# A two-stage attention and token-mixing kernel: token mix in two column parts, q loaded first, the root on Pool in the first batch, mixers turned at landing, and a new timetable

## The chip, the cores and the metric

The kernel runs on one core of one Trainium2 chip. The metric is the device time of one execution in microseconds (us). "PE" is TensorE's matmul stream, "DVE" is VectorE, "ACT" is ScalarE, and "POOL" is GpSimd.

## The reference, cut to what matters

```python
# attention without softmax: B = 8, H = 8, S = 576, D = 64
kv  = einsum('bhsd,bhse->bhde', k, v)
out = einsum('bhsd,bhde->bhse', q, kv)
x   = out / sqrt(mean(out**2, -1) + 1e-6) * g_norm      # then (B, S, 512)
# mixing of phases
theta = x @ w_theta
y  = w_tok_r @ (x * cos(theta)) + w_tok_i @ (x * sin(theta))   # over the 576 tokens
u  = x + y
result = u + maximum(u @ w_ch, 0)
```

## The kernel before

Each batch goes through seven stages. They are written as generators. A list of start times and steps (the timetable) sorts their pieces by a nominal time, and each engine gets its instructions in exactly that order. The nominal times themselves are never waited for, so the timetable is nothing but an order for each engine's queue.

```python
START = [8.0, 38.0, 60.0] + [86.0 + 26.0 * i for i in range(5)]
STEPS = {                      # stage: (offset from the batch's start, step from tile to tile)
    "cast": (-1.0, 3.4), "attention": (0.0, 3.4), "norm": (16.0, 5.2), "turn": (24.0, 5.2),
    "phase": (28.0, 5.2), "mix": (54.0, 3.25), "channel": (82.0, 5.2),
    # ... own entries for the first batch
}
PS = {"kv": 1, "raw": 2, "tp": 2, "mm": 3}            # PSUM banks by use
```

The stages that the argument needs, cut:

```python
def norm(b, ti):                 # one tile of 128 tokens, 5 tiles (the last of 64)
    # PE: raw (PSUM) ...; ACT: sq = raw**2; then
    nc.vector.reduce_sum(out=ss, in_=sq)
    if b > 0:                    # first batch: one chain of 13 instructions on VectorE, for all tiles
        nc.gpsimd.tensor_scalar(out=ss, in0=ss, scalar1=D * eps, op0=ALU.add)
        nc.gpsimd.tensor_tensor(out=rt, in0=ss, in1=mhalf, op=ALU.pow)
    yield 2.8
    nc.vector.tensor_tensor(out=x, in0=raw, in1=rt, op=ALU.mult)

def phase(b, ti):                # PE: th = x @ w_theta; ACT: pt; DVE: f, fa; ACT: tr = sin; DVE: z
    ...

def mix(b, i):                   # 8 groups of 9 matmuls
    (kc, half) = divmod(i, 2)    # the half (288 of 576 tokens) is the inner loop
    # PE: y (PSUM, "mm"); DVE: uT = y * g + xT, for 128 channels and one half
    ...

def channel(b, ti):              # needs uT of all 512 channels for tile ti
    # PE: ups (transpose) and vps = u @ w_ch ("mm"); ACT: u; DVE: ot = max(vps, 0) + u; store
    ...
```

Because the half is the inner loop of the mix, no channel tile can run before the seventh of the eight mix groups. The middle tile straddles both halves and needs all eight.

Of the kernel before, what the change touches and what calls it, by code (L numbers as in the profile page):

```python
# [10 lines left out]
FP32 = mybir.dt.float32  # L11
# [8 lines left out]
START = [8.0, 38.0, 60.0] + [86.0 + 26.0 * i for i in range(5)]  # L20
STEPS = {
    "cast": (-1.0, 3.4),
    "attention": (0.0, 3.4),
    "norm": (16.0, 5.2),
    "turn": (24.0, 5.2),
    "phase": (28.0, 5.2),
    "mix": (54.0, 3.25),
    "channel": (82.0, 5.2),

    ("norm", 0): (14.5, 0.4),  # L30
    ("turn", 0): (22.0, 0.9),
    ("phase", 0): (24, 1.2),
    ("mix", 0): (36.0, 2.6),
    ("channel", 0): (60.0, 4.0),
}

# [18 lines left out]
def kernel(  # L55
# [31 lines left out]
    SH = S // 2  # L87
# [51 lines left out]
    loaded = {}  # L139

    def load(b):
# [3 lines left out]
        for hp in range(HP):  # L145
# [4 lines left out]
            for (dst, src) in ((kt, k), (vt, v), (qt, q)):  # L150
                nc.sync.dma_start(
                    out=dst[:].rearrange("p h j d -> p h (j d)"),
                    in_=src[b, pair, 0:SF, :].rearrange("h (p j) d -> p h (j d)", j=NF),
                )
# [33 lines left out]
    def cast_theta(kc):  # L188
        nc.scalar.activation(out=wth[:, kc, :], in_=wst_t[kc][:], func=AFT.Copy, scale=FOLD)

    def mixer_tails():
        for i in range(2):
            nc.gpsimd.tensor_copy(wtt[:, 0:NF, i, :], wnat[i][:, :, SF:S])
            nc.gpsimd.tensor_copy(wtt[:T, NF, i, :], wnatl[i][:, SF:S])

    def load_mixers():

        nc.gpsimd.tensor_copy(late[:], loaded[0][2][HP - 1][:, 0, 0, 0:1])  # L198
        for (i, src) in ((0, moe_w_tok_r), (1, moe_w_tok_i)):
# [3 lines left out]
            nc.gpsimd.dma_start(out=wnatl[i][:], in_=src[SF:S, :])  # L203
        nc.gpsimd.dma_start(out=wch[:], in_=moe_w_ch.rearrange("(k p) c -> p k c", p=P))

    def mixer_step(n):

        pw = ps("tp", [P, S], FP16, f"wTps{n}")
        for tj in range(NT):
            rows = P if tj < NF else T  # L210
            if n < 2 * NF:
                i = n // NF
                src = wnat[i][:, tj, :] if tj < NF else wnatl[i][:, :]
                st = src[:, bass.ds(n % NF, P, NF)]
            else:
                st = wtt[:rows, tj, :, :]
            nc.tensor.matmul(  # L217
                pw[:, tj * P:tj * P + rows], st, ident16[:rows, :rows],
# [11 lines left out]
    st = {}  # L230

    def cast_q(b, hp):
# [5 lines left out]
        if hp == 0:  # L238
            nc.vector.tensor_copy(qc[:T, NF], ql[:])
        yield 0  # L240

    def attention(b, hp):
        (ks, vs, qs, kl, vl, ql) = loaded[b]
        if hp == 0:
            st["kv", b] = ps("kv", [P, HP, D], FP32, f"kv{b}")
        kvp = st["kv", b]
        pair = slice(2 * hp, 2 * hp + 2)
# [8 lines left out]
        pq = ps("tp", [P, SX], FP16, f"qTps{b}_{hp}")  # L256
        for j in range(NT):
            nc.tensor.matmul(  # L258
                pq[:, j * P:(j + 1) * P], qcast[b % 2][:, j, pair, :], ident16[:],
                is_transpose=True, start=(j == 0), stop=(j == NT - 1),  # L260
            )
        yield 2.0
        t = work.tile([P, S], FP16, tag="qT", bufs=2 * HP, name=f"qT{b}_{hp}")
        nc.scalar.copy(out=t[:], in_=pq[:, 0:S])  # L264
# [9 lines left out]
    def rsqrt(rt, ss, n):  # L274

        i = work.tile([P, n], I32, tag="rs_i", name="rs_i")
        h = work.tile([P, n], FP32, tag="rs_h", name="rs_h")
        w = work.tile([P, n], FP32, tag="rs_w", name="rs_w")
        nc.vector.tensor_scalar(
            out=ss, in0=ss, scalar1=D * eps, scalar2=None, op0=ALU.add  # L280
        )
        nc.vector.tensor_scalar(
            out=i[:], in0=ss.bitcast(I32), scalar1=1, scalar2=None,
            op0=ALU.logical_shift_right,
        )
        nc.vector.tensor_scalar(
            out=rt.bitcast(I32), in0=i[:], scalar1=-1, scalar2=0x5F3759DF,
            op0=ALU.mult, op1=ALU.add,
        )
        nc.vector.tensor_scalar(  # L290
            out=h[:], in0=ss, scalar1=-0.5, scalar2=None, op0=ALU.mult
        )
        for _ in range(3):
            nc.vector.tensor_tensor(out=w[:], in0=rt, in1=rt, op=ALU.mult)
            nc.vector.tensor_tensor(out=w[:], in0=w[:], in1=h[:], op=ALU.mult)
            nc.vector.scalar_tensor_tensor(
                out=rt, in0=w[:], scalar=1.5, in1=rt, op0=ALU.add, op1=ALU.mult
            )

    def norm(b, ti):  # L300


        first = b == 0
        bd = kv_bd[b % 2]
        raw = ps("mm" if first and ti >= 2 else "raw", [P, C], FP32, f"raw{b}_{ti}")
# [14 lines left out]
        if ti == 0 or not first:  # L320
            n = NT if first else 1
            tag = "0" if first else ""
            st["ss", b] = work.tile(
                [P, n, H], FP32, tag="ss" + tag, bufs=4 - 3 * first, name=f"ss{b}_{ti}"
            )
            st["rt", b] = work.tile(
                [P, n, H], FP32, tag="rt" + tag, bufs=4 - 3 * first, name=f"rt{b}_{ti}"
            )
        ss, rt, at = st["ss", b], st["rt", b], ti if first else 0
        nc.vector.reduce_sum(  # L330
            out=ss[:, at], in_=sq[:].rearrange("p (h e) -> p h e", h=H),
            axis=mybir.AxisListType.X,
        )
        if not first:
            nc.gpsimd.tensor_scalar(  # L335
                out=ss[:, 0], in0=ss[:, 0], scalar1=D * eps, scalar2=None, op0=ALU.add
            )
            nc.gpsimd.tensor_tensor(out=rt[:, 0], in0=ss[:, 0], in1=mhalf[:], op=ALU.pow)  # L338
            yield 2.8
        else:  # L340
            if ti == NT - 1:
# [188 lines left out]
```

## Time and profile before

| | before |
|---|---|
| time, median of 3 | 266.01 us (264.6 to 266.35) |
| profiled span | 265.8 us |
| PE, DVE, ACT, POOL busy | 226.2, 192.4, 165.4, 77.3 us |

These are lines of the page of the kernel before. The first has busy time, share and count of instructions. The next two have 40 equal slices of the span, with PE's busy share and the granted PE clock in tenths. The last has the shares of the chain that ended last, by engine.

```profile
PE 226.2 (85%) x2253; PEld 153.3 (58%) x2253; DVE 192.4 (72%) x408; ACT 165.4 (62%) x291; POOL 77.3 (29%) x88
...
PE   1472886998867798899999998999899979889993
PEclk9999997799999999999999999999999999999999
...
PE 35%; DVE 28%; POOL 13%; ACT 9%; DMA 6%; issue 6%; SPq 1%; POOLq 1%; ACTq 0%; DVEq 0%
```

The fill, the first 60 us or so, has the holes.

The next lines are busy times by stage. A stage ends when another batch's worth of mix matmuls (72) has been issued; the first ends at the first batch's first mix group, and the ninth at the last matmul. The columns are the window, its length, busy us (with instructions) of PE, PEld (weight loads), DVE, ACT and POOL, then the granted clock, the DMA share and GB/s.

```profile
0.00:47.50 47.50, 27.47 (x260) 19.49 (x261) 25.51 (x70) 23.59 (x41) 6.64 (x18) 0.96 1.04 263
47.50:88.40 40.90, 34.89 (x405) 23.93 (x405) 26.75 (x54) 26.37 (x47) 14.92 (x16) 0.97 0.47 144
88.40:111.50 23.10, 19.50 (x207) 13.21 (x204) 20.19 (x45) 16.32 (x29) 9.91 (x10) 1.00 0.99 269
111.50:135.70 24.20, 23.94 (x266) 16.99 (x265) 20.34 (x43) 18.33 (x32) 9.83 (x10) 1.00 0.21 70
135.70:163.30 27.60, 27.38 (x287) 18.55 (x285) 22.73 (x48) 19.93 (x37) 10.15 (x10) 1.00 0.63 182
163.30:190.50 27.20, 26.27 (x281) 18.12 (x277) 22.97 (x48) 19.66 (x36) 10.15 (x10) 1.00 0.62 175
190.50:216.80 26.30, 25.36 (x254) 16.98 (x252) 22.08 (x45) 19.43 (x36) 9.51 (x10) 1.00 0.14 46
216.80:240.70 23.90, 21.00 (x165) 13.17 (x162) 19.59 (x40) 15.40 (x27) 6.16 (x7) 1.00 0.15 50
240.70:261.00 20.30, 20.22 (x153) 12.87 (x152) 11.52 (x20) 6.38 (x11) 0.00 (x0) 1.00 0.30 101
```

The Trainium skill says, in "Perfetto Trace Analysis", "Per-instruction lifecycle": the end of a matmul is estimated by the profiler and not observed. For this reason I count **lost** time as the length of a stage less its work at dense pace. The dense paces are read from start to start of groups in the timeline: mix group of 288 columns 1.10 us; theta or channel group 0.86; k-v group 0.73; transposes of q 0.37, of a mixer 0.46, others 0.22; raw 0.22.

The first batch's norm on VectorE, from its timeline (start, length, engine, line, operation):

```profile
22.66 0.68 DVE L330 TENSOR_REDUCE ss_0_287<-sq_4_302 128x8 f32<-128x512 f32 x1
...
26.36 0.69 DVE L346 TENSOR_TENSOR x_0_327<-raw_0_261,rt_0_288 128x512 f16<-128x512 f32 x1
...
31.54 0.69 DVE L382 SCALAR_TENSOR_TENSOR f_0_379<-pt_0_371,th_0_355 128x512 f32<-128x512 f32 x1 [2.10 <-ACT pt_0_371 L379]
```

The chain of 13 small instructions, cut here, stands between the last reduce and the first x at 26.36 us; it starts at 23.37 us. The first f comes at 31.54 us.

### The profile page before, as it was taken

To read this page: it belongs to the slowest core of one execution; us is meant where nothing else is said; L and a number is where in the kernel's file an instruction comes from. 1 tells how busy PE (TensorE), PEld (TensorE's weight loads), DVE (VectorE), ACT (ScalarE), POOL (GpSimd) and SP (SyncE) were. 2 spreads that over 40 slices of the span, in tenths; PEclk is the share of its full clock that TensorE was granted. 3 is DMA by queue.
4 is the path that set the end of the run, shared out by engine and by line. 5 is a ranking of instruction groups with operands and counts; after the bars stand their busy time and mean duration, and the time that the engine had idled before them with its cause. 6 is when DMAs were issued, how large, how long until landed. Compare 5 with 4: busy or idle time off the path is not lost.

```text
span 265.8 us, 5776 instructions
## 1 busy us (share of the span) xinstructions
PE 226.2 (85%) x2253; PEld 153.3 (58%) x2253; DVE 192.4 (72%) x408; ACT 165.4 (62%) x291; POOL 77.3 (29%) x88
## 2 busy tenths in 40 slices
PE   1472886998867798899999998999899979889993
PEld 1361455686534575577667665767666646556651
DVE  5118567347688978887978789778987888786552
ACT  2146496234997798378856885688568857752231
POOL 2051000023553353532252423343334423500000
PEclk9999997799999999999999999999999999999999
DMA  5999999886221899631239911993121112122234
GB/s 158 284 362 211 247 343 224 274 234 206 78 79 42 198 313 257 205 120 42 79 112 247 316 43 43 229 333 111 41 62 42 41 39 61 40 79 62 79 100 141
DMA packets 45676, 41.04 MB, mean 154 GB/s; under 512 B 15056, under 2 KB 40272, under 8 KB 45648
## 3 DMA queue, kind: packets, MB, share of 16 engines
q1 hardware_dynamic: 44608, 38.81, 50.4%
q0 software_dynamic: 1040, 1.85, 3.7%
q8 instruction: 18, 0.29, 0.5%
q14 instruction: 10, 0.08, 0.1%
HBM read 33.06 MB, written 9.44 MB: 160 GB/s over the span
## 4 chain that ended last, share of the span: by engine, by line
PE 35%; DVE 28%; POOL 13%; ACT 9%; DMA 6%; issue 6%; SPq 1%; POOLq 1%; ACTq 0%; DVEq 0%
DMA ql_111<-in_q_dram 2%; DMA v_3_134<-in_v_dram 2%; DMA out_dram<-ot_0_2607 1%; DVE ss_0_287 L330 1%; PE kv_463 L250 1%; PE y_0_604 L420 1%; PE kv_1985 L250 1%; PE kv_1522 L250 1%; POOL rt_4_1365 L338 1%; DVE uT_2529 L425 1%; POOL rt_3_2640 L338 1%; POOL rt_1_2883 L338 1%; POOL rt_1_1486 L338 1%; POOL rt_1_2416 L338 1%; POOL rt_4_1009 L338 1%
## 5 line engine op out<-in xcount | busy, mean ns | idle before, releaser
L335 POOL TENSOR_SCALAR ss_0_704<-ss_0_704 128x8 f32<-128x8 f32 x1 | 0.2, 240 | 27.7 <-DVE ss_0_704 L330 27.7
L258 PEld LDWEIGHTS <-qcast_75 128*128 128x128 f16 x80 | 5.3, 106 | 3.3 <-DVE qcast_75 L235 1.6
L258 PEld LDWEIGHTS <-qcast_77 128*128 128x128 f16 x80 | 4.8, 100 | 4.0 <-DVE qcast_77 L235 2.9
L359 PE MATMUL xTps_0_338<-ident_79,x_0_327 128*128 128x128 f16 x4 | 0.6, 305 | 5.7 <-DVE x_0_327 L346 5.7
L250 PE MATMUL kv_155<-vl_68,kl_67 128*64 128x64 f32 x16 | 1.8, 319 | 3.6 <-DMA vl_68<-in_v_dram 3.6
L250 PE MATMUL kv_155<-v_0_113,k_0_112 128*64 128x64 f32 x16 | 1.1, 319 | 4.3 <-DMA v_0_113<-in_v_dram 4.3
L264 ACT COPY qT_0_200<-qTps_0_166 128x576 f16<-128x576 f16 x1 | 0.6, 639 | 6.6 <-PE qTps_0_166 L258 6.6
L198 POOL COPY late<-q_3_135 128x1 f32<-128x1 f32 x1 | 0.4, 438 | 13.6 <-DMA q_3_135<-in_q_dram 13.6
L359 PEld LDWEIGHTS <-x_0_327 128*128 128x128 f16 x4 | 0.3, 130 | 5.9 <-DVE x_0_327 L346 5.9
L250 PEld LDWEIGHTS kv_155<-vl_68,kl_67 128*64 128x64 f32 x16 | 1.4, 222 | 3.7 <-issue 3.7
L250 PEld LDWEIGHTS kv_155<-v_0_113,k_0_112 128*64 128x64 f32 x16 | 1.0, 222 | 4.3 <-DMA k_0_112<-in_k_dram 4.3
L373 PEld LDWEIGHTS <-xT_337 128*128 128x128 f16 x20 | 2.2, 120 | 2.1 <-issue 1.1
L330 DVE TENSOR_REDUCE ss_0_287<-sq_0_271 128x8 f32<-128x512 f32 x1 | 0.7, 686 | 3.6 <-ACT sq_0_271 L318 3.6
L373 PEld LDWEIGHTS <-xT_3332 128*128 128x128 f16 x20 | 1.9, 98 | 2.2 <-issue 0.9
L364 ACT ACTIVATE xT_337<-xTps_0_338,gcol 128x512 f16<-128x512 f16 x1 | 0.7, 687 | 3.4 <-PE xTps_0_338 L359 3.4
L217 PEld LDWEIGHTS <-wnat_107 128*128 128x128 f16 x16 | 1.5, 123 | 2.3 <-issue 2.1
L373 PEld LDWEIGHTS <-xT_1108 128*128 128x128 f16 x20 | 1.8, 98 | 1.6
L373 PEld LDWEIGHTS <-xT_2426 128*128 128x128 f16 x20 | 1.9, 98 | 1.3
L373 PEld LDWEIGHTS <-xT_2893 128*128 128x128 f16 x20 | 1.9, 98 | 1.3
L373 PEld LDWEIGHTS <-xT_1496 128*128 128x128 f16 x20 | 1.9, 98 | 1.3
L373 PEld LDWEIGHTS <-xT_1954 128*128 128x128 f16 x20 | 1.9, 98 | 1.3
L441 PEld LDWEIGHTS <-uT_1584 128*128 128x128 f16 (+1 forms) x20 | 1.8, 100 | 1.4 <-issue 0.2
(1950 smaller groups left out, 985.6 us busy)
## 6 DMA issues: line engine op xcount, KB each, us to landing
wnat_106<-in_moe_w_tok_r_dram POOLq DMA_DIRECT2D x1, 576.0 KB, 8.6
wnat_107<-in_moe_w_tok_i_dram POOLq DMA_DIRECT2D x1, 576.0 KB, 10.9
kl_67<-in_k_dram SPq DMA_DIRECT2D x4, 128.0 KB, 5.2
vl_68<-in_v_dram SPq DMA_DIRECT2D x4, 128.0 KB, 5.5
kl_71<-in_k_dram SPq DMA_DIRECT2D x4, 128.0 KB, 5.5
vl_72<-in_v_dram SPq DMA_DIRECT2D x4, 128.0 KB, 6.5
wch<-in_moe_w_ch_dram POOLq DMA_DIRECT2D x1, 512.0 KB, 13.8
k_0_112<-in_k_dram SPq DMA_DIRECT2D x1, 256.0 KB, 2.8
```

The costliest lines, as they stand in the source:

```text
L217: nc.tensor.matmul(pw[:, tj * P:tj * P + rows], st, ident16[:rows, :rows], is_transpose=True, start=(tj == 0), stop=(tj == NT - 1),)
L250: nc.tensor.matmul(kvp[r * D:(r + 1) * D, hp, :], ks[hp][:, r, j, :] if j < NF else kl[:, 2 * hp + r, :], vs[hp][:, r, j, :] if j < NF els ...
L258: nc.tensor.matmul(pq[:, j * P:(j + 1) * P], qcast[b % 2][:, j, pair, :], ident16[:], is_transpose=True, start=(j == 0), stop=(j == NT - 1),)
L264: nc.scalar.copy(out=t[:], in_=pq[:, 0:S])
L330: nc.vector.reduce_sum(out=ss[:, at], in_=sq[:].rearrange("p (h e) -> p h e", h=H), axis=mybir.AxisListType.X,)
L338: nc.gpsimd.tensor_tensor(out=rt[:, 0], in0=ss[:, 0], in1=mhalf[:], op=ALU.pow)
L359: nc.tensor.matmul(px[:, kc, :], st["x", b, ti][:, kc * P:(kc + 1) * P], ident16[:], is_transpose=True, start=(kc == 0), stop=(kc == NK - 1),)
L364: nc.scalar.activation(out=st["xT", b][:, :, ti * P:(ti + 1) * P], in_=px[:], func=AFT.Copy, scale=gcol[:],)
L373: nc.tensor.matmul(th[:], xT[:, kc, ti * P:(ti + 1) * P], wth[:, kc, :], start=(kc == 0), stop=(kc == NK - 1),)
L420: nc.tensor.matmul(y[:], st["z", b, m][:, kc * P:(kc + 1) * P], wT[m][:, cols], start=(m == 0), stop=(m == 2 * NF),)
L425: nc.vector.scalar_tensor_tensor(out=st["uT", b][:, kc, cols], in0=y[:], scalar=gcol[:], in1=st["xT", b][:, kc, cols], op0=ALU.mult, op1=A ...
L441: nc.tensor.matmul(vp[:rows], uT[:, kc, ti * P:ti * P + rows], wch[:, kc, :], start=(kc == 0), stop=(kc == NK - 1),)
```

## The change

The intent, as the diff shows it, is to let channel tiles of a batch run before its mix is complete (first the columns of 256 tokens for all channels, then those of 320), to shorten the first batch's start, and to give all queues a new order. The core of the diff:

```diff
-START = [8.0, 38.0, 60.0] + [86.0 + 26.0 * i for i in range(5)]
+START = [8.0, 33.0, 54.1, 80.3, 106.3, 132.5, 158.4, 184.5]
 STEPS = {
-    "cast": (-1.0, 3.4), "attention": (0.0, 3.4), "norm": (16.0, 5.2), "turn": (24.0, 5.2),
-    "phase": (28.0, 5.2), "mix": (54.0, 3.25), "channel": (82.0, 5.2),
+    "cast": (-3.73, 2.84), "attention": (-0.20, 3.37), "norm": (16.34, 5.20), "turn": (23.12, 5.34),
+    "phase": (27.31, 5.11), "mix": (54.00, 3.16), "channel": (70.95, 4.96),
+    ("channel", 0): (47.00, 4.14), ("channel", 1): (59.52, 5.04),   # ... and more for batches 0 and 1
 }
+MIXERS = (17.68, 1.09)            # the mixers' turns stood at 28.0, 0.8
@@ mix
-    SH = S // 2
+    SH = 2 * P
-        (kc, half) = divmod(i, 2)
+        (half, kc) = divmod(i, NK)
@@ load and attention
-            for (dst, src) in ((kt, k), (vt, v), (qt, q)):
+            for (dst, src) in ((qt, q), (kt, k), (vt, v)):
 # the transposes of q stand ahead of the k-v products; the first batch's last qT copy goes to DVE
@@ norm: the chain of 13 instructions on VectorE is removed; add and power on Pool for all batches
@@ Wch
+        landed(1)                 # a copy on Pool that waits for the second batch's last v
         nc.gpsimd.dma_start(out=wch[:], ...)
```

More of the change, by code (lines that the diff above doesn't have):

```diff
@@ L15 @@
 ALU = mybir.AluOpType
-START = [8.0, 38.0, 60.0] + [86.0 + 26.0 * i for i in range(5)]
+START = [8.0, 33.0, 54.1, 80.3, 106.3, 132.5, 158.4, 184.5]
 STEPS = {
-    "cast": (-1.0, 3.4),
-    "attention": (0.0, 3.4),
-    "norm": (16.0, 5.2),
-    "turn": (24.0, 5.2),
-    "phase": (28.0, 5.2),
-    "mix": (54.0, 3.25),
-    "channel": (82.0, 5.2),
-    ("norm", 0): (14.5, 0.4),
-    ("turn", 0): (22.0, 0.9),
-    ("phase", 0): (24, 1.2),
-    ("mix", 0): (36.0, 2.6),
-    ("channel", 0): (60.0, 4.0),
+    "cast": (-3.73, 2.84),
+    "attention": (-0.20, 3.37),
+    "norm": (16.34, 5.20),
+    "turn": (23.12, 5.34),
+    "phase": (27.31, 5.11),
+    "mix": (54.00, 3.16),
+    "channel": (70.95, 4.96),
+    ("cast", 0): (-0.52, 2.20),
+    ("attention", 0): (0.95, 2.20),
+    ("norm", 0): (9.96, 0.69),
+    ("turn", 0): (14.32, 1.61),
+    ("phase", 0): (16.00, 2.19),
+    ("mix", 0): (32.42, 2.68),
+    ("channel", 0): (47.00, 4.14),
+    ("cast", 1): (-5.70, 2.32),
+    ("attention", 1): (-3.78, 2.33),
+    ("norm", 1): (10.04, 3.81),
+    ("turn", 1): (17.00, 3.34),
+    ("phase", 1): (19.50, 3.83),
+    ("mix", 1): (40.00, 3.74),
+    ("channel", 1): (59.52, 5.04),
 }
+MIXERS = (17.68, 1.09)
 def in_traced_order(tc):
@@ L139 @@
     loaded = {}
+    st = {}
     def load(b):
@@ L189, in cast_theta @@
         nc.scalar.activation(out=wth[:, kc, :], in_=wst_t[kc][:], func=AFT.Copy, scale=FOLD)
+        st["wth", kc] = wth[:, kc, :]
     def mixer_tails():
@@ L194, in mixer_tails, with landed @@
             nc.gpsimd.tensor_copy(wtt[:T, NF, i, :], wnatl[i][:, SF:S])
+        st["wtt"] = wtt
+    def landed(b):
+        nc.gpsimd.tensor_copy(late[:], loaded[b][1][HP - 1][:, 0, 0, 0:1])
     def load_mixers():
-        nc.gpsimd.tensor_copy(late[:], loaded[0][2][HP - 1][:, 0, 0, 0:1])
+        landed(0)
         for (i, src) in ((0, moe_w_tok_r), (1, moe_w_tok_i)):
@@ L203, in load_mixers, with load_channel @@
             nc.gpsimd.dma_start(out=wnatl[i][:], in_=src[SF:S, :])
+    def load_channel():
+        landed(1)
         nc.gpsimd.dma_start(out=wch[:], in_=moe_w_ch.rearrange("(k p) c -> p k c", p=P))
+        st["wch"] = wch
     def mixer_step(n):
@@ L213, in mixer_step @@
                 src = wnat[i][:, tj, :] if tj < NF else wnatl[i][:, :]
-                st = src[:, bass.ds(n % NF, P, NF)]
+                src = src[:, bass.ds(n % NF, P, NF)]
             else:
-                st = wtt[:rows, tj, :, :]
+                src = st["wtt"][:rows, tj, :, :]
             nc.tensor.matmul(
-                pw[:, tj * P:tj * P + rows], st, ident16[:rows, :rows],
+                pw[:, tj * P:tj * P + rows], src, ident16[:rows, :rows],
                 is_transpose=True, start=(tj == 0), stop=(tj == NT - 1),
@@ L226, in mixer_step @@
         wT.append(t)
-    st = {}
     def cast_q(b, hp):
@@ L239, in cast_q @@
             nc.vector.tensor_copy(qc[:T, NF], ql[:])
+        st["qc", b, hp] = qc
         yield 0
@@ L243, in attention @@
         (ks, vs, qs, kl, vl, ql) = loaded[b]
+        pair = slice(2 * hp, 2 * hp + 2)
+        pq = ps("tp", [P, SX], FP16, f"qTps{b}_{hp}")
+        for j in range(NT):
+            nc.tensor.matmul(
+                pq[:, j * P:(j + 1) * P], st["qc", b, hp][:, j, pair, :], ident16[:],
+                is_transpose=True, start=(j == 0), stop=(j == NT - 1),
+            )
         if hp == 0:
@@ L246, in attention @@
         kvp = st["kv", b]
-        pair = slice(2 * hp, 2 * hp + 2)
         for j in range(NT):
@@ L255, in attention @@
                 )
-        pq = ps("tp", [P, SX], FP16, f"qTps{b}_{hp}")
-        for j in range(NT):
-            nc.tensor.matmul(
-                pq[:, j * P:(j + 1) * P], qcast[b % 2][:, j, pair, :], ident16[:],
-                is_transpose=True, start=(j == 0), stop=(j == NT - 1),
-            )
         yield 2.0
         t = work.tile([P, S], FP16, tag="qT", bufs=2 * HP, name=f"qT{b}_{hp}")
-        nc.scalar.copy(out=t[:], in_=pq[:, 0:S])
+        if b == 0 and hp == HP - 1:
+            nc.vector.tensor_copy(t[:], pq[:, 0:S])
+        else:
+            nc.scalar.copy(out=t[:], in_=pq[:, 0:S])
         st["qT", b, hp] = t
@@ L272, in attention @@
                 )
-    def rsqrt(rt, ss, n):
-        i = work.tile([P, n], I32, tag="rs_i", name="rs_i")
-        h = work.tile([P, n], FP32, tag="rs_h", name="rs_h")
-        w = work.tile([P, n], FP32, tag="rs_w", name="rs_w")
-        nc.vector.tensor_scalar(
-            out=ss, in0=ss, scalar1=D * eps, scalar2=None, op0=ALU.add
-        )
-        nc.vector.tensor_scalar(
-            out=i[:], in0=ss.bitcast(I32), scalar1=1, scalar2=None,
-            op0=ALU.logical_shift_right,
-        )
-        nc.vector.tensor_scalar(
-            out=rt.bitcast(I32), in0=i[:], scalar1=-1, scalar2=0x5F3759DF,
-            op0=ALU.mult, op1=ALU.add,
-        )
-        nc.vector.tensor_scalar(
-            out=h[:], in0=ss, scalar1=-0.5, scalar2=None, op0=ALU.mult
-        )
-        for _ in range(3):
-            nc.vector.tensor_tensor(out=w[:], in0=rt, in1=rt, op=ALU.mult)
-            nc.vector.tensor_tensor(out=w[:], in0=w[:], in1=h[:], op=ALU.mult)
-            nc.vector.scalar_tensor_tensor(
-                out=rt, in0=w[:], scalar=1.5, in1=rt, op0=ALU.add, op1=ALU.mult
-            )
     def norm(b, ti):
-        first = b == 0
         bd = kv_bd[b % 2]
-        raw = ps("mm" if first and ti >= 2 else "raw", [P, C], FP32, f"raw{b}_{ti}")
+        raw = ps("mm" if b == 0 and ti >= 2 else "raw", [P, C], FP32, f"raw{b}_{ti}")
         for hp in range(HP):
@@ L319, in norm @@
         yield 0.9
-        if ti == 0 or not first:
-            n = NT if first else 1
-            tag = "0" if first else ""
-            st["ss", b] = work.tile(
-                [P, n, H], FP32, tag="ss" + tag, bufs=4 - 3 * first, name=f"ss{b}_{ti}"
-            )
-            st["rt", b] = work.tile(
-                [P, n, H], FP32, tag="rt" + tag, bufs=4 - 3 * first, name=f"rt{b}_{ti}"
-            )
-        ss, rt, at = st["ss", b], st["rt", b], ti if first else 0
+        ss = work.tile([P, H], FP32, tag="ss", bufs=4, name=f"ss{b}_{ti}")
         nc.vector.reduce_sum(
-            out=ss[:, at], in_=sq[:].rearrange("p (h e) -> p h e", h=H),
+            out=ss[:], in_=sq[:].rearrange("p (h e) -> p h e", h=H),
             axis=mybir.AxisListType.X,
         )
-        if not first:
-            nc.gpsimd.tensor_scalar(
-                out=ss[:, 0], in0=ss[:, 0], scalar1=D * eps, scalar2=None, op0=ALU.add
-            )
-            nc.gpsimd.tensor_tensor(out=rt[:, 0], in0=ss[:, 0], in1=mhalf[:], op=ALU.pow)
-            yield 2.8
-        else:
-            if ti == NT - 1:
-                rsqrt(rt[:].rearrange("p n h -> p (n h)"),
-                      ss[:].rearrange("p n h -> p (n h)"), NT * H)
-            yield 4.0 - 0.4 * ti
+        nc.gpsimd.tensor_scalar(
+            out=ss[:], in0=ss[:], scalar1=D * eps, scalar2=None, op0=ALU.add
+        )
+        rt = work.tile([P, H], FP32, tag="rt", bufs=4, name=f"rt{b}_{ti}")
+        nc.gpsimd.tensor_tensor(out=rt[:], in0=ss[:], in1=mhalf[:], op=ALU.pow)
+        yield 2.8
         x = work.tile([P, C], FP16, tag="x", bufs=NT + 4, name=f"x{b}_{ti}")
@@ L348, in norm @@
             in0=raw[:].rearrange("p (h e) -> p h e", h=H),
-            in1=rt[:, at].unsqueeze(2).broadcast_to((P, H, D)),
+            in1=rt[:].unsqueeze(2).broadcast_to((P, H, D)),
             op=ALU.mult,
@@ L367, in turn_x @@
         )
+        st["xTb", b, ti] = st["xT", b][:, :, ti * P:(ti + 1) * P]
     def phase(b, ti):
-        xT = st["xT", b]
+        xT = st["xTb", b, ti]
         th = ps("mm", [P, C], FP32, f"th{b}_{ti}")
@@ L373, in phase @@
             nc.tensor.matmul(
-                th[:], xT[:, kc, ti * P:(ti + 1) * P], wth[:, kc, :],
+                th[:], xT[:, kc, :], st["wth", kc],
                 start=(kc == 0), stop=(kc == NK - 1),
@@ L413, in mix @@
     def mix(b, i):
-        (kc, half) = divmod(i, 2)
+        (half, kc) = divmod(i, NK)
         if i == 0:
             st["uT", b] = work.tile([P, NK, S], FP16, tag="uT", bufs=2, name=f"uT{b}")
-        cols = slice(half * SH, (half + 1) * SH)
-        y = ps("mm", [P, SH], FP32, f"y{b}_{i}")
+        cols = slice(SH, S) if half else slice(0, SH)
+        y = ps("mm", [P, S - SH if half else SH], FP32, f"y{b}_{i}")
         for m in range(2 * NF + 1):
@@ L428, in mix @@
         )
+        st["u", b, half, kc] = st["uT", b][:, kc, :]
     def channel(b, ti):
-        uT = st["uT", b]
         rows = P if ti < NF else T
+        uT = [st["u", b, int(ti * P >= SH), kc][:, ti * P:ti * P + rows] for kc in range(NK)]
         pu = ps("tp", [P, C], FP16, f"ups{b}_{ti}")
@@ L435, in channel @@
             nc.tensor.matmul(
-                pu[:rows, kc * P:(kc + 1) * P], uT[:, kc, ti * P:ti * P + rows],
+                pu[:rows, kc * P:(kc + 1) * P], uT[kc],
                 ident16[:], is_transpose=True, start=(kc == 0), stop=(kc == NK - 1),
@@ L441, in channel @@
             nc.tensor.matmul(
-                vp[:rows], uT[:, kc, ti * P:ti * P + rows], wch[:, kc, :],
+                vp[:rows], uT[kc], st["wch"][:, kc, :],
                 start=(kc == 0), stop=(kc == NK - 1),
@@ L479 @@
     for kc in range(NK):
-        put(START[0] + 17.0 + 0.1 * kc, once(cast_theta, kc))
-    put(START[0] + 27.0, once(mixer_tails))
+        put(START[0] + STEPS["phase", 0][0] - 1.0 + 0.2 * kc, once(cast_theta, kc))
+    put(START[0] + 20.0, once(mixer_tails))
+    put(START[1] + 4.0, once(load_channel))
     for m in range(2 * NF + 1):
-        put(START[0] + 28.0 + 0.8 * m, once(mixer_step, m))
+        put(START[0] + MIXERS[0] + MIXERS[1] * m, once(mixer_step, m))
     for b in range(B):
```

## The prediction

> **What bounds it now.** From about 50 us on, TensorE's instruction stream. The page shows PE busy 85% of 265.8 us; its slices are mostly 9 tenths late, 1 to 8 in much of the fill. Counting dense paces from the timeline (mix group of nine matmuls 1.10 us, theta or channel group of four 0.865, k-v group 0.73, four or five transposes 0.23 to 0.31), all PE work is about 203 us. The first mix group starts at 47.5 us with 188 us of it left, and the last matmul ends at 261: 26 us lost after that point, 9 of them before the second batch's first mix group (88.4 us), later 2 to 3 us per batch of 25 us. A 4.7 us tail follows. The fill is worth most.
>
> **What moves in the fill.**
> - First norm. Before: five reduces, then a 13-instruction VectorE chain (23.4 to 26.3 us), first x at 26.36, all five by 29.4. After: Pool adds and powers per tile; one costs 0.24 + 1.68 us, about 2.05 with its gap. First x near 23.3, but the five then come at Pool's pace, the last near 31: VectorE's order puts the first f behind it, so the first f stays near 31.5.
> - q first: last k-v group still waits for the last landing (15.7 us); one ScalarE copy before the k-v copies goes away. About 0.5 us.
> - Wch (1 MB) leaves the first 40 us, where the DMA share is 1.1; I estimate batch 1's loads land 3 us sooner (near 37 instead of 40).
> - The mixers' nine turns and batch 1's whole attention now stand among the theta groups, ahead of the first mix group. Before, the turns stalled at 40 to 47 us, with a clock record of 0.67, and two attention groups came after. The Trainium skill ("TensorE: Matmul & The Clock Gate", Part 1) says an idle array drops to half clock; the trace agrees: that mix group ran at 240 ns per matmul against 122 later.
>
> VectorE's work after the last x sums to about 11.5 us: first mix group near 44.5 us (42 to 47), 186 us left, 5 us ahead in all. Batch 1's norm follows at once, so the second batch's first mix group should come near 73 us with 160 left (before: 88.4, 156).
>
> **Steady state and drain.** Mix columns 256 + 320 cost the same as 2 x 288: 107+2.5 and 133+2.5 ns estimated from 122 for 288; weight loads of 100 ns still hide. Part-major order lets channel tiles 0 and 1 start after half the mix; PE was already full there: maybe 0 to 2 us, minus a bubble near 1 us before the last three channel tiles.
>
> **Sum.** 73 + 160 + about 15 lost (before 16) + 4.7 = 253; one more for stalls at closer packing: **254 us**, 80% range 248 to 260. Faster by over 2%: 0.90; within 2%: 0.08; slower: 0.02.
>
> **Right if:** first x 22.5 to 24 us; first mix group at 42 to 47; second batch's at 70 to 76; PE slices of 9 from slice 8 on; PE work unchanged, DVE busy down 3 us, POOL up 10; span between later batches' mix starts 26 to 27.5 us.
>
> **Wrong if:** Pool's pace or late b1 loads stall PE so the first mix group is past 47 (then 257 to 262); the clock drops again in the fill; VectorE, 23 of 27 us busy per batch, becomes the limit at the tighter spacing; or steady batches shrink to 25.5 us (then under 248).

## The result, and the profile after

| | before | changed | ratio |
|---|---|---|---|
| time, median of 4 | 266.18 us | 247.82 us (247.41 to 248.29) | 0.9316, 95% interval 0.9267 to 0.9365 |
| profiled span | 265.8 us | 244.7 us | |
| PE, DVE, ACT, POOL busy | 226.2, 192.4, 165.4, 77.3 | 217.7, 190.8, 165.9, 83.8 us | |

Ratios are the mean time of one kernel's runs over the mean time of the other's runs of the same rounds, so they are not quite the ratios of the medians quoted.

The prediction of 254 us with a range from 248 to 260 was 6 us too high, and the measured median lies just below the range. Device time lies above the span, by 1.8 to 3.2 us in the four runs of the changed kernel, and the prediction's sum ends with the span. In like terms it was 8 to 9 us too high: about 254 against spans of 244.7 to 246.0 us.

The same lines of the page, for the changed kernel:

```profile
PE 217.7 (89%) x2253; PEld 150.2 (61%) x2253; DVE 190.8 (78%) x396; ACT 165.9 (68%) x290; POOL 83.8 (34%) x99
...
PE   0771898889996899999999999999999999999993
PEclk9997599999999999999999999999999999999998
...
PE 66%; DVE 14%; POOL 7%; DMA 4%; ACT 4%; issue 2%; SPq 1%; ACTq 0%; DVEq 0%
```

The chain that ended last is now on PE for 66%. The stages, cut in the same way:

```profile
0.00:43.20 43.20, 26.73 (x310) 18.71 (x311) 23.72 (x58) 24.88 (x43) 15.81 (x29) 0.88 1.06 273
43.20:72.40 29.20, 26.43 (x283) 18.06 (x282) 21.82 (x45) 20.35 (x38) 10.03 (x10) 1.00 0.77 210
72.40:103.20 30.80, 27.89 (x310) 19.34 (x310) 26.48 (x55) 22.36 (x40) 14.01 (x14) 1.00 0.49 147
103.20:126.50 23.30, 23.30 (x261) 16.75 (x260) 21.68 (x47) 19.02 (x35) 9.53 (x10) 1.00 0.69 192
126.50:152.10 25.60, 25.60 (x278) 17.91 (x277) 23.36 (x49) 20.06 (x36) 9.63 (x10) 1.00 0.63 189
152.10:177.60 25.50, 25.50 (x278) 17.96 (x277) 22.89 (x48) 19.92 (x36) 9.52 (x10) 1.00 0.66 187
177.60:201.90 24.30, 24.30 (x252) 16.96 (x251) 21.86 (x44) 19.81 (x35) 9.53 (x10) 1.00 0.14 46
201.90:221.40 19.50, 19.50 (x157) 12.86 (x156) 18.09 (x38) 14.15 (x25) 5.72 (x6) 1.00 0.18 62
221.40:240.30 18.90, 18.20 (x138) 11.63 (x135) 10.20 (x18) 5.33 (x9) 0.00 (x0) 1.00 0.24 85
```

From the fourth to the eighth stage PE is busy for the whole of each window. Lost time by stage, in us, from these windows and the dense paces; the last column is the sum from the second batch's first mix group on:

| stage | 1 fill | 2 | 3 | 4 | 5 | 6 | 7 | 8 | 9 | 3 to 9 |
|---|---|---|---|---|---|---|---|---|---|---|
| before | 30.1 | 9.1 | 4.8 | 0.8 | 1.3 | 2.0 | 2.2 | 3.9 | 0.7 | 15.7 |
| changed | 23.6 | 3.8 | 4.0 | 0.3 | 0.3 | 0.3 | 0.2 | 0.4 | 1.4 | 6.9 |

The first two stages came out as predicted: the first mix group at 43.2 us (predicted 44.5) and the second batch's at 72.4 us (predicted 73). The miss lies in the stages behind.

The norm of the first batch, VectorE's timeline and then Pool's for one tile:

```profile
17.62 0.69 DVE L314 TENSOR_REDUCE ss_0_279<-sq_0_265 128x8 f32<-128x512 f32 x1 [2.63 <-ACT sq_0_265 L311]
...
21.04 0.68 DVE L325 TENSOR_TENSOR x_0_324<-raw_0_260,rt_0_282 128x512 f16<-128x512 f32 x1
...
28.73 0.69 DVE L325 TENSOR_TENSOR x_4_354<-raw_4_298,rt_4_322 128x512 f16<-128x512 f32 x1 [1.38 <-POOL rt_4_322 L322]
29.34 0.68 DVE L362 SCALAR_TENSOR_TENSOR f_0_377<-pt_0_356,th_0_346 128x512 f32<-128x512 f32 x1
```

```profile
20.49 0.24 POOL L318 TENSOR_SCALAR ss_1_291<-ss_1_291 128x8 f32<-128x8 f32 x1
20.81 1.67 POOL L322 TENSOR_TENSOR rt_1_294<-ss_1_291,mhalf 128x8 f32<-128x8 f32 x1
```

The first x comes at 21.04 us and the second at 22.52, then one every 2.07 us at Pool's pace (0.24 + 1.67 us and two small gaps). The last comes at 28.73. The first f stands behind it in the queue, as the prediction said, and comes at 29.34 us.

One caution: the profiled execution was an early one. In a second profile of the same kernel (e18 below) the first batch's data landed 1.1 us later, with the first x at 22.17 and the first mix group at 44.2 us. So the fill column of the tables is good to about 1.5 us. The other columns of those two profiles agree to 0.2 us. The spread of the fill is that of the landing: from the start of the first batch's last k-v group to the first mix group it is 28.2 us in this profile and 28.1 in e18 (31.8 in the kernel before). I use this stretch below to compare fills.

### The profile page after: what moved, and what is told of

It is laid out like the page before. It is cut to its first block, busy times and chain, and to the rows that moved or that the text cites. A ratio compares the mean times of both kernels' runs of the same rounds, so it can differ in the third digit from the quotient of the medians.

```text
span 244.7 us, 5763 instructions
## 1 busy us (share of the span) xinstructions
PE 217.7 (89%) x2253; PEld 150.2 (61%) x2253; DVE 190.8 (78%) x396; ACT 165.9 (68%) x290; POOL 83.8 (34%) x99
## 4 chain that ended last, share of the span: by engine, by line
PE 66%; DVE 14%; POOL 7%; DMA 4%; ACT 4%; issue 2%; SPq 1%; ACTq 0%; DVEq 0%
DMA v_3_134<-in_v_dram 3%; DMA q_1_123<-in_q_dram 2%; PE kv_2043 L274 1%; PE kv_2977 L274 1%; PE kv_2508 L274 1%; PE kv_1591 L274 1%; PE kv_447 L274 1%; DVE uT_1121 L406 1%; SPq L167 1%; PE th_0_346 L353 1%; POOL rt_1_703 L322 1%; PE th_1_372 L353 1%; POOL rt_0_1115 L322 1%; POOL rt_0_677 L322 1%; POOL rt_0_282 L322 1%
## 5 line engine op out<-in xcount | busy, mean ns | idle before, releaser
L265 PEld LDWEIGHTS <-qcast_75 128*128 128x128 f16 x80 | 5.9, 105 | 10.2 <-DVE qcast_75 L252 6.8
L265 PE MATMUL qTps_0_154<-ident_79,qcast_75 128*128 128x128 f16 x5 | 0.9, 304 | 7.8 <-DVE qcast_75 L252 6.4
L265 PEld LDWEIGHTS <-qcast_77 128*128 128x128 f16 x80 | 5.6, 97 | 2.7 <-issue 0.9
L353 PEld LDWEIGHTS <-xT_326 128*128 128x128 f16 x20 | 1.8, 111 | 3.8 <-ACT wth L199 1.8
L338 PE MATMUL xTps_0_327<-ident_79,x_0_324 128*128 128x128 f16 x4 | 0.6, 308 | 3.8 <-DVE x_0_324 L325 3.8
L353 PE MATMUL th_0_346<-wth,xT_326 128*128 128x512 f16 x4 | 1.9, 622 | 1.6 <-DVE x_2_338 L325 1.6
L353 PEld LDWEIGHTS <-xT_716 128*128 128x128 f16 x20 | 1.9, 97 | 1.7
L338 PEld LDWEIGHTS <-x_0_324 128*128 128x128 f16 x4 | 0.3, 132 | 4.0 <-DVE x_0_324 L325 4.0
L353 PEld LDWEIGHTS <-xT_1567 128*128 128x128 f16 x20 | 1.8, 98 | 1.6 <-issue 0.4
L353 PEld LDWEIGHTS <-xT_3367 128*128 128x128 f16 x20 | 1.9, 98 | 1.4
L429 ACT COPY u_0_3855<-ups_0_3844 128x512 f16<-128x512 f16 x1 | 0.6, 586 | 3.1 <-PE ups_0_3844 L417 3.1
L353 PEld LDWEIGHTS <-xT_1996 128*128 128x128 f16 x20 | 1.8, 98 | 1.2
L353 PEld LDWEIGHTS <-xT_2463 128*128 128x128 f16 x20 | 1.8, 98 | 1.2
L423 PEld LDWEIGHTS <-uT_3733 128*128 128x128 f16 (+1 forms) x20 | 1.8, 100 | 1.2
L423 PEld LDWEIGHTS <-uT_1121 128*128 128x128 f16 (+1 forms) x20 | 1.8, 100 | 1.2
L423 PEld LDWEIGHTS <-uT_2096 128*128 128x128 f16 (+1 forms) x20 | 1.8, 100 | 1.2
```

The source lines that it names most:

```text
L265: nc.tensor.matmul(pq[:, j * P:(j + 1) * P], st["qc", b, hp][:, j, pair, :], ident16[:], is_transpose=True, start=(j == 0), stop=(j == NT ...
L338: nc.tensor.matmul(px[:, kc, :], st["x", b, ti][:, kc * P:(kc + 1) * P], ident16[:], is_transpose=True, start=(kc == 0), stop=(kc == NK - 1),)
L353: nc.tensor.matmul(th[:], xT[:, kc, :], st["wth", kc], start=(kc == 0), stop=(kc == NK - 1),)
L423: nc.tensor.matmul(vp[:rows], uT[kc], st["wch"][:, kc, :], start=(kc == 0), stop=(kc == NK - 1),)
L429: nc.scalar.copy(out=u[:rows], in_=pu[:rows])
```

## The experiments

The rival theories at first were these. A: the new order of the queues (the timetable) makes the gain by itself. B: the changed operations make it, above all the part-major mix. Each kernel ran three timed rounds beside the kernel before on the same chip (the last two, five rounds). All results were correct. Differences in us below are between medians of different series, on different chips. The changed kernel had 247.82 and 248.00 us on two chips; the kernel before had medians from 266.18 to 267.88, so the ratios give somewhat smaller differences.

| run | what | median us | ratio to before (95%) |
|---|---|---|---|
| changed kernel | | 247.82 | 0.9316 (0.9267 to 0.9365) |
| e1 | new operations, old timetable | 268.97 | 1.0071 (0.9998 to 1.0144) |
| e2 | old operations, new timetable | 256.95 | 0.9622 (0.9572 to 0.9672) |
| e3 | old mix, and channel late as it must be | 255.88 | 0.9573 (0.9516 to 0.9629) |
| e4 | first root on VectorE | 249.67 | 0.9346 (0.9298 to 0.9394) |
| e5 | k first | 250.70 | 0.9370 (0.9319 to 0.9420) |
| e6 | mixers late | 256.16 | 0.9588 (0.9550 to 0.9626) |
| e7 | Wch early | 247.74 | 0.9282 (0.9244 to 0.9319) |
| e8 | channel late, all batches | 255.38 | 0.9558 (0.9504 to 0.9613) |
| e9 | e8, and x further back | 258.69 | 0.9714 (0.9648 to 0.9780) |
| e10 | three changes of the fill | 246.45 | 0.9254 (0.9199 to 0.9310) |
| e11 | dummy matmuls | 247.69 | 0.9302 (0.9242 to 0.9363) |
| e12 | two changes of order in the fill | 247.49 | 0.9301 (0.9226 to 0.9377) |
| e13 | e8, channel later still | 256.55 | 0.9578 (0.9543 to 0.9612) |
| e14 | channel 1.55 later | 253.84 | 0.9484 (0.9447 to 0.9520) |
| e15 | channel late, first two batches | 252.22 | 0.9413 (0.9355 to 0.9471) |
| e16 | channel late, last three | 250.83 | 0.9376 (0.9341 to 0.9411) |
| e17 | roots shared by Pool and VectorE | 247.26 | 0.9273 (0.9227 to 0.9319) |
| e18 | changed kernel again | 248.00 | 0.9295 (0.9253 to 0.9337) |

Lost time by stage, in us, of the runs that the argument uses:

| stage | 1 fill | 2 | 3 | 4 | 5 | 6 | 7 | 8 | 9 |
|---|---|---|---|---|---|---|---|---|---|
| e1 new operations, old timetable | 29.3 | 11.5 | 4.6 | 0.8 | 1.3 | 1.7 | 1.7 | 4.2 | 0.8 |
| e2 old operations, new timetable | 23.5 | 5.0 | 6.2 | 2.3 | 0.8 | 0.9 | 0.6 | 3.4 | 0.7 |
| e3 old mix | 24.2 | 4.0 | 5.6 | 1.7 | 1.0 | 0.6 | 0.4 | 3.4 | 0.7 |
| e8 channel late | 25.0 | 4.2 | 5.5 | 1.6 | 0.6 | 0.3 | 0.3 | 3.4 | 0.9 |
| e9 e8, x further back | 23.7 | 4.2 | 7.0 | 2.0 | 2.0 | 2.0 | 1.7 | 2.1 | 0.9 |
| e13 channel later, in step | 25.0 | 4.2 | 6.6 | 1.7 | 2.1 | 1.2 | 1.2 | 0.4 | 0.4 |
| e14 channel early, out of step | 23.7 | 3.8 | 4.0 | 1.2 | 1.3 | 1.3 | 1.1 | 3.1 | 0.6 |
| e15 late in the first two | 25.2 | 4.2 | 6.6 | 1.1 | 0.3 | 0.3 | 0.2 | 0.4 | 1.2 |
| e16 late in the last three | 24.9 | 3.8 | 4.0 | 0.3 | 0.3 | 0.3 | 0.4 | 3.5 | 0.9 |
| e18 changed kernel again | 24.5 | 3.8 | 4.0 | 0.3 | 0.3 | 0.3 | 0.2 | 0.4 | 1.2 |

### e1 and e2: operations and timetable apart

e1 takes the changed kernel's operations and the old timetable:

```diff
-START = [8.0, 33.0, 54.1, ...]   # and all new STEPS, MIXERS
+START = [8.0, 38.0, 60.0] + [86.0 + 26.0 * i for i in range(5)]   # and all old STEPS
+MIXERS = (28.0, 0.8)
```

> All code of the changed kernel (parts of 256 and 320, part-major; q first; power on Pool; Wch held), but the timetable (all starts and steps, the mixers too) of the kernel before. Theory A, the timetable makes the gain (it decides the order in which instructions stand on each in-order engine): 260 to 266 us, and 2 to 3 us lost on PE per steady batch as before. Theory B, the changed operations make it, above all the part-major mix: 245 to 253 us.

Measured: 268.97 us, even a little above the expected 266, with an interval that just contains 1. Its stages are those of the kernel before, but for 2.4 us more lost in the second. The changed operations bring nothing under the old order.

e2 is the reverse:

```diff
+    SH = S // 2; (kc, half) = divmod(i, 2)       # old mix; k first; root on VectorE; Wch with the mixers
-    "channel": (70.95, 4.96), ("channel", 0): (47.00, 4.14), ("channel", 1): (59.52, 5.04),
+    "channel": (78.00, 4.96), ("channel", 0): (53.00, 4.14), ("channel", 1): (68.00, 5.04),
```

> The reverse: operations as before (two halves of 288 with the half as the inner loop, k first, root on VectorE for the first batch, Wch loaded with the mixers), timetable of the changed kernel, with the channel steps put 6 to 8.5 later because they must follow the whole mix. Theory A: 247 to 253 us, second batch's first mix group at 72 to 76 us, under 1 us lost per steady batch. Theory B: 257 to 265 us.

Measured: 256.95 us, which is neither theory's number. The timetable alone brings 3.8%, mostly in the first two stages. The remaining 3 points of the gain need the operations and the timetable together.

### e3 and e8: the part-major mix, and the place that it frees for the channel

e3 undoes only the mix order, so its channel steps must stand behind the whole mix:

```diff
-    SH = 2 * P;   (half, kc) = divmod(i, NK)
+    SH = S // 2;  (kc, half) = divmod(i, 2)
     # channel steps late, as in e2
```

> The changed kernel with only the part-major mix undone (halves of 288, half as the inner loop, channel steps 6 to 8.5 later). Theory A (order of the rest): within 2 us of the changed kernel, 246 to 250 us. Theory B (part-major spreads the channel work of VectorE and ScalarE): the steady batches lose 2 us each again, 256 to 262 us.

Measured: 255.88 us. Theory A falls for this part: 8 of the 18 us hang on the mix order. But B's detail is wrong too: stages 4 to 7 lose 1.4, 0.7, 0.3 and 0.2 us more than in the changed kernel, not 2 each. e8 keeps the part-major mix and only moves the channel steps late:

```diff
-    "channel": (70.95, 4.96), ("channel", 0): (47.00, 4.14), ("channel", 1): (59.52, 5.04),
+    "channel": (78.00, 4.96), ("channel", 0): (53.00, 4.14), ("channel", 1): (68.00, 5.04),
```

> The changed kernel, part-major mix kept, but its channel steps put 6 to 8.5 later, where the kernel with the old mix had to have them. Theory B1, part-major pays because it lets the channel tiles stand earlier in the queues: back to the old mix's 254 to 257 us. Theory B2, the part-major mix pays by itself: 247 to 249 us.

Measured: 255.38 us. The interval overlaps that of e3 almost wholly, and the stages agree. The part-major mix is worth nothing in itself that these runs show. It is worth 7.6 us (255.38 less 247.82) because it makes an earlier place for the channel legal. Of this, 5.7 us are lost time from the third stage on (12.6 against 6.9).

### e15 and e16: in which batches

```diff
# e15: late channel steps for batches 0 and 1 only;  e16: for batches 5, 6 and 7 only
```

> The changed kernel with late channel steps for the first two batches alone (6 and 8.5 later). In the late version 1.5 us more were lost from the second to the third batch's mix and 1.3 from the third to the fourth's: 249.5 to 251.5 us if that comes from these two batches' steps, 247.5 to 248.5 us if it comes from the later ones.

> The changed kernel with late channel steps for the last three batches alone. In the late version 3.0 us more were lost between the last two batches' first mix groups, where no further batch fills PE: 250 to 251.5 us, and no more than 0.5 us per batch before. If the end is not special: 248 to 249 us.

Measured: 252.22 and 250.83 us, that is 4.4 and 3.0 us above the changed kernel; together 7.4 of e8's 7.6. e15 was a little more costly than expected. So the early channel pays at both ends. In the middle batches PE is full whether it stands early or late: e8 loses 0.6, 0.3 and 0.3 us in stages 5 to 7, the changed kernel 0.3, 0.3 and 0.2.

### e9, e13 and e14: why

In e8, VectorE waited 10.8 us in all in front of 21 x for Pool's power (from the third batch's mix to the last one's); in the changed kernel there was no such wait in that stretch. VectorE's timeline shows why. First e8, in its eighth stage:

```profile
212.69 0.68 DVE L314 TENSOR_REDUCE ss<-sq 128x8 f32<-128x512 f32 x1
213.28 0.68 DVE L362 SCALAR_TENSOR_TENSOR f<-pt,th 128x512 f32<-128x512 f32 x1
214.00 0.43 DVE L374 TENSOR_SCALAR fa<-f 128x512 int32<-128x512 int32 x1
214.34 0.48 DVE L406 SCALAR_TENSOR_TENSOR uT<-y,gcol,xT 128x256 f16<-128x256 f32 x1
215.48 0.69 DVE L325 TENSOR_TENSOR x<-raw,rt 128x512 f16<-128x512 f32 x1 [0.66 <-POOL rt L322]
216.09 0.75 DVE L390 TENSOR_TENSOR z<-x,tr 128x512 f16<-128x512 f16 x2
```

Between the reduce (ss) and the x of the same tile stand f, fa and uT, about 1.5 us of work (213.28 to 214.82). Pool needs 2.1 us to answer. So VectorE idles 0.66 us in front of x, although the first z behind x had its tr since 214.63 us. The ot behind them, at 216.76 us, could not have filled this wait: ACT copied its u only from 215.15 to 215.72 us. The Trainium skill says of VectorE's queue that it is strict FIFO ("TensorE: Matmul & The Clock Gate", "Architectural detail"), and this is what that looks like in a trace. Now the changed kernel in the same stage:

```profile
206.91 0.68 DVE L314 TENSOR_REDUCE ss_3_3498<-sq_3_3495 128x8 f32<-128x512 f32 x1
207.50 0.68 DVE L362 SCALAR_TENSOR_TENSOR f_1_3533<-pt_1_3503,th_1_3490 128x512 f32<-128x512 f32 x1
208.21 0.43 DVE L374 TENSOR_SCALAR fa_1_3535<-f_1_3533 128x512 int32<-128x512 int32 x1
208.55 0.69 DVE L432 SCALAR_TENSOR_TENSOR ot_3_3537<-vps_3_3515,u_3_3531 128x512 f32<-128x512 f32 x1
209.15 0.48 DVE L406 SCALAR_TENSOR_TENSOR uT_3421<-y_2_3520,gcol,xT_2930 128x256 f16<-128x256 f32 x1
209.70 0.69 DVE L325 TENSOR_TENSOR x_3_3545<-raw_3_3481,rt_3_3501 128x512 f16<-128x512 f32 x1
```

Here ot stands between the reduce and the x, and x starts without a wait. The channel step as a whole comes earlier in the tile's cycle, so the u of this ot was ready at 208.30 us.

e9 tests this in the simplest way, by putting x further back in e8:

```diff
-        yield 2.8
+        yield 4.4 if b >= 2 else 2.8          # before x
```

> The version with late channel steps (255.4 us), and in addition x put 1.6 later behind its power on VectorE's queue, for the third batch on. In the late-channel version VectorE waits 10.8 us for Pool's power in front of 21 x, between the third batch's first mix group and the last one's; in the changed kernel never. If that wait is the cause (only 1.8 us of VectorE work stands between a reduce and its x, against 2.1 us of Pool's answer): the wait goes under 3 us and the time to 248 to 251 us, without the early channel. If the channel's place counts for another reason (PSUM banks, ScalarE): still 254 us or more.

Measured: 258.69 us, slower than e8. The wait on Pool did vanish, but x then came too late for PE, which showed a new wait (line of PE's waits of e9 from the third batch's mix on; us in total, times, longest):

```profile
PE xTps L338 <- DVE x L325: 6.6, 10, 1.3
```

My simple theory falls: the wait on Pool alone is not the cost. In the middle batches (stages 4 to 7) e8 had 17 such waits, 8.2 us in all, and lost 2.8 us there (the changed kernel 1.1); moving x back put the delay where PE could not cover it. e13 and e14 separate two better ones. C: the output's place within a tile's cycle counts. D: how early the channel comes counts.

```diff
# e13: e8, with
+    "channel": (81.20, 4.96),      # later than 78.00, but ot stands between reduce and x again
# e14: the changed kernel, with
+    "channel": (72.50, 4.96),      # early, but ot stands behind x
```

> The version with late channel steps (255.4 us), with the steps from the third batch on another 3.2 later. VectorE's order is then again as in the changed kernel: each output instruction between a reduce and its x, not behind the x. Theory C, the place of the output within the tile's cycle counts (it fills Pool's answer time of 2.1 us): the x wait on Pool goes under 3 us and the time to 250 to 253 us, in spite of a deeper pipeline. Theory D, how early the channel comes counts (the pipeline's depth): 255.5 to 258 us.

> The changed kernel with channel steps 1.55 later from the third batch on, still before the end of the mix: each output instruction now stands behind its x. Theory C: VectorE waits for Pool's power again (8 us or more) and the time goes to 251 to 255 us. Theory D: 247.5 to 249 us.

Measured: 256.55 us for e13 (as D expected) and 253.84 us for e14 (as C expected). Neither theory holds for all stages, but by stage they separate cleanly. In the eighth stage, where no new batch brings PE other work, the versions with the new timetable and ot behind x (e2, e3, e8, e14, e16; early or late) lost 3.1 to 3.5 us, and those with ot in front of it (changed kernel, e13, e15, e18) lost 0.4. e9 stands apart: its x moved back and did not wait for Pool, but PE's transposes waited 1.3 us for x, and it lost 2.1. VectorE's wait line in that stage, for e8:

```profile
DVE x L325 <- POOL rt L322: 2.6, 4, 0.7
```

e14 and e16 have the same 2.6 us in four waits; e13 and the changed kernel have none. In e8 the chain of waits from 206 to 221 us runs over VectorE, ACT and Pool and nowhere over PE. So for the end of the program C is shown, as far as it says that the channel's place in the tile's cycle counts. Each of these runs moves the whole channel step (PE's two groups, ACT's copy of u, and ot), so that ot on VectorE is the part that matters is read from the waits and was not tested alone. In the middle batches both e13 and e14 lose 1 to 2 us per batch, in different waits of PE, in stages 4 to 7. First e13, then e14:

```profile
PE ups L417 <- ACT xT L343: 2.3, 3, 0.8
PE y L401 <- DVE z L390: 1.4, 2, 0.7
```

```profile
PE y L401 <- DVE ot L432: 2.9, 6, 0.8
```

e13's channel transposes wait on ACT for xT copies to leave (both use the two "tp" banks); e14's mix groups wait until a late ot frees a bank (both use the three "mm" banks). In e14 the ot is late because of C again: in these stages 14 x waited for Pool, 6.6 us in all, and the chain that leads to a late mix group runs through Pool's power, the x that waited for it and the ot behind that x (start, length):

```profile
172.64 1.68 POOL rt L322
174.34 0.07 DVE x L325
175.70 0.61 DVE ot L432
176.35 1.38 PE y L401 x9
```

Moving the channel by 1.55 nominal us out of the changed kernel's place costs 6 us. Not every other place costs that in the middle batches: e8's, 7 nominal us later, loses hardly more than the changed kernel's in stages 5 to 7. When a wait of VectorE reaches PE is read here from wait lines and was not tested bank by bank.

### e4, e5, e6, e7: the parts of the fill

```diff
# e4: the 13-instruction chain on VectorE for the first batch's root again
# e5: load order k, v, q; k-v products ahead of q's transposes; last qT copy on ACT again
# e6: MIXERS = (28.00, 0.80); ("mix", 0): (36.00, 2.60); ("channel", 0): (50.00, 4.14)
# e7: Wch loaded right behind the mixers, no wait for the second batch
```

> The changed kernel with the first batch's root back on VectorE in one chain of 13 instructions. First x comes later (near 23.8 us instead of 21.0), the fifth earlier (near 26.9 instead of 29.4), so the first f can come 2 us sooner. If the first x is what counts: 249 to 251 us. If the last x and the first f count (my reading of VectorE's order): 245 to 248 us. Either way no more than 3 us of the 18.

> The changed kernel with k, v, q as load order and k-v products ahead of the transposes of q. If the order only moves the first batch's start: first mix group 0.5 to 1 us later, 248 to 249.5 us. If it also matters in each steady batch (a transpose that waits for its cast stops PE sooner): over 250 us.

> The changed kernel with the mixers turned late, behind the theta groups, as before. PE's holes between 22 and 32 us stay empty and 4 us of turns (9 of 0.46) come later: first mix group 2 to 4 us later, 250 to 252 us. If the turns are free either way, 247 to 248.5 us.

> The changed kernel with Wch loaded with the mixers. Batch 1's loads land about 3 us later (last v near 39 instead of 36 us); its last k-v group runs at 42.4, so there is slack: 247.5 to 249 us. If the slack is used up: 250 us or more.

Measured: 249.67, 250.70, 256.16 and 247.74 us. The root on Pool is worth 1.9 us (1.4 in the stretch from the last k-v group to the first mix group, 29.5 against 28.1 us): with the chain, the first x came at 25.27 us, with the first f about where it was in e18 (30.82 against 30.47), so the gain does not come through the first f. That it comes from PE's earlier start is my reading and was not tested. q first is worth 2.9 us, more than my half microsecond in the prediction (for e4 and e5 the intervals of the ratios still overlap that of the changed kernel); e5 also lost 5.4 us in the second stage against 3.8, and 0.5 to 0.6 in each middle batch against 0.3. The mixers' place is worth 8.3 us, more than twice what I expected: e6's first mix group came at 51.5 us, with the granted clock at 0.50 from 45 to 50 us. (The first mix and channel steps had to move back with the turns, so this is the price of the whole rearrangement.) Holding Wch back is worth nothing that these runs show. These prices hold for the changed kernel alone and don't add up elsewhere: e2 has k first, the old root and the early Wch on top of e3's old mix, and is only 1.1 us slower than e3 on the same chip.

### e10, e11, e12, e17, e18: what still bounds the fill

```diff
# e11: 50 dummy matmuls (256 columns) on PE: 30 behind the first batch's raw groups, 10 behind each of
#      the first two xTps
# e12: theta casts ahead of the first xT on ACT; the first f ahead of the fifth x on VectorE
# e10: e11 and e12 together
# e17: e11, the theta casts of e12, and the roots of tiles 3 and 4 by a chain of 13 on VectorE
# e18: the changed kernel, unaltered
```

> The changed kernel with the 50 dummy matmuls alone. The clock record of 0.50 to 0.60 at 20 to 30 us goes to 0.9 or more, theta groups take 0.86 instead of 1.7 us. If PE bounds that stretch: 2 to 3 us sooner, 244.5 to 246 us. If Pool and VectorE bound it: 247 to 248 us.

> The changed kernel with only the two changes of order (theta casts before the first xT, first f before the fifth x). First theta group 1 us sooner, first f near 27.5 instead of 29.3 us: 246 to 247 us. If nothing else follows sooner: 247.5 to 248.5 us.

> The changed kernel with three changes of the first batch: theta casts ahead of the first xT on ScalarE, the first f ahead of the fifth x on VectorE, and 50 dummy matmuls in PE's holes from 17.8 to 25.4 us so that the clock stays up. First mix group at 39 to 42 us instead of 43.2: 243 to 246.5 us. If the fill is bound by Pool's pace of 2.07 us per power: 247 us or more.

> The changed kernel with theta casts ahead of the first xT, the 50 dummy matmuls, and the roots of the first batch's tiles 3 and 4 on VectorE (one chain of 13 on 16 columns, about 2.5 us) while Pool does the power for tiles 0 to 2. If Pool's five powers in a row (10.3 us) bound the fill: fifth x 9 to 10.5 us after the first reduce ends instead of 11, first mix group 1 to 2 us sooner than in the changed kernel of the same call, 245 to 246.5 us. If the fill is bound by ScalarE's and PE's queue behind it: within 0.5 us of the changed kernel.

> The changed kernel unaltered, as the measure for the run beside it on the same chip: 247.5 to 248.5 us, and how much the first mix group's start varies from one profile to another (43.2 us in its first profile, 44.0 to 44.8 in others with the same instructions up to there).

e11: 247.69 us, no gain, although the clock did what was wanted. The window from 20 to 30 us of the changed kernel, then of e11 (columns as in the stage windows; PE busy counts the dummies):

```profile
20.00:30.00 10.00, 5.79 (x26) 2.84 (x27) 4.72 (x8) 5.25 (x9) 9.06 (x13) 0.55 1.10 240
```

```profile
20.00:30.00 10.00, 8.54 (x76) 6.18 (x75) 4.71 (x8) 5.76 (x11) 9.33 (x10) 1.00 1.11 228
```

The granted clock is 1.00 instead of 0.55, the first theta group shows 1.02 us busy instead of 1.87, and the first mix group comes no sooner (44.0 us; e18 44.2). Raising PE's half clock in that stretch gained nothing, because PE then waited for the x that Pool's powers set free. e12 (247.49) and e10 (246.45) sit at or just under the changed kernel. e17 (0.9273) against e18 (0.9295), on one chip, is 0.2% apart with intervals that overlap nearly wholly, so sharing the roots did not show a gain either. e10 has the lowest median of all, 1.4 us under the changed kernel, but it was not timed in the same series as that kernel, so I do not call it faster. The profiles say a little more. From the last k-v group to the first mix group e11 and e12 took 28.1 us, like the changed kernel, but e17 took 27.3 and e10, which is e11 and e12 together, 26.9. So neither the clock nor the order of f and theta casts is the limit alone, and the two together gain 1.2 us. What bounds the 24 us that the fill still loses is left open.

## Why the prediction was right or wrong

- **The fill's numbers were right.** The step "first mix group near 44.5 us" measured 43.2 and 44.2 in two profiles, and "73 with 160 left" measured 72.4, with about 161 us of work at the dense paces. The reasons given hold in part: the mixers' turns were the largest item (8.3 us in e6), the root on Pool 1.9, q first 2.9 (predicted 0.5), Wch nothing in time (the landing was predicted 3 us sooner). The 44.5 was in part luck: it was reckoned from VectorE's work after the last x, but in e4 the last x ended 2.2 us sooner than in e18 (28.35 against 30.55 us) and the first mix group came 1.8 us later (46.0 against 44.2; 1.4 counted from the landing).
- **The step that failed** is the term "about 15 lost (before 16)" behind the second batch's first mix, with its reason in the paragraph on steady state: "Part-major order lets channel tiles 0 and 1 start after half the mix; PE was already full there: maybe 0 to 2 us". That term measured 6.9 us. The prediction's 15 is what the versions with the channel in its old place behind the mix do lose from there on: 14.9 in e2, 13.4 in e3, 12.6 in e8. So the early channel, put at 0 to 2 us, is worth 5.7 us of lost time in these stages and 7.6 us of the time (e8). With the "one more for stalls at closer packing", which did not come either, this term is the miss of 8 to 9 us in the span; the other terms of the sum were right within about 1 us (72.4 for 73, 161 for 160, a tail of 4.4 for 4.7). That device time lies about 2 us above the span, which the sum left out, brought the number nearer to the result by luck.
- **Why I mis-sized it.** I took PE for full ("PE was already full there") and treated 2 to 3 us per batch as a price of the matmul stream. The chain of waits of the kernel before said otherwise: 35% on PE, 41% on DVE and POOL; in the changed kernel it is 66% on PE. I also judged the channel's place by PE's work alone. Its effect, as the waits show it, came over VectorE's queue: whether ot stands in front of an x that waits for Pool.
- **Mechanism, as far as shown.** At the end of the program it is the channel's place in the tile's cycle, with ot between reduce and x (3 us). In the middle, the two other places of e13 and e14 cost 1 to 2 us per batch, by their wait lines through banks held too long; e8's place cost little. The 4.4 us of the first two batches are measured (e15), but the chain of causes inside them was not taken apart and stays open.
- **Smaller points.** First x predicted 22.5 to 24, measured 21.0 and 22.2. DVE was to be busy 3 us less and was 1.6 less; POOL 10 more and was 6.5 more. "PE slices of 9 from slice 8 on" held from slice 15 on, but for the last. "Mix starts 26 to 27.5 us apart" was wrong: 25.5, the case named under "wrong if" as "under 248".
- The half clock in the fill was rightly read from the trace (though 0.67 is the record of 40 to 50 us; from 40 to 47 us it is 0.74). What the trace shows there is the half speed; it shows no long idle stretch of PE, whose longest marked wait from 38 to 47.5 us was 1.5 us. Lifting it alone gained nothing in the changed kernel (e11).

## What to carry to other kernels

When a kernel is only an order of in-order queues, cost a change of order by what each queue holds between a request and its answer: fill a two-microsecond answer from another engine with an instruction that is ready, and check that no bank is held longer for it. Before calling a matmul stream full, compare its length with its work at dense pace, and look at whose time the chain that ended last is made of. A rewritten loop can be worth nothing in itself and still pay, by making a better order legal; test the two apart.

## What the Trainium skill lacked or had wrong

- "GPSIMD Engine Reference" gives no cost for a power: 128 x 8 fp32 took 1.67 us on Pool here, against 0.24 us for the addition of a constant to the same shape, and a row of them ran at one per 2.07 us.
- "TensorE: Matmul & The Clock Gate", Part 1, "HAM oscillation" tells to keep the clock up by leaving no long gaps. Here dummy matmuls did raise the record from 0.55 to 1.00 in the fill, and the time did not change (247.69 against 247.82 us). The page does not say to check first that PE bounds that stretch.
- "Perfetto Trace Analysis" says that matmul ends are estimated and that matmul busy time is a bad metric, but gives no figure for what can hide in it: a stage marked busy for 27.38 of 27.60 us had 1.3 us lost, and the kernel before lost 15.7 us from the second batch's mix on with most slices at 9 tenths.
- I found no page on the place of an instruction within an in-order queue relative to an answer it does not need: a shift of 1.55 nominal us of one stage cost 6 us (e14).
